# Two token groups share one pass over the gated layer's weights, the sign is set as a bit, and gate weights stay out of DRAM

## The chip, the cores and the metric

The kernel runs on one core of a Trainium2 chip. The metric is device time in microseconds (us), median of several runs. Before the change: 1014.65 us (three runs, 1012.99 to 1016.63).

## The reference, cut to what matters

Three layers follow each other on 4 x 576 = 2304 tokens of width 512: a causal attention with decay (8 heads of 64), a gated layer (SwiGLU, inner width 1536), and a top-1 mixture of 8 experts (inner width 1024).

```python
scores = where(causal, -1e9, q @ k.T / sqrt(64) + cum[:, None] - cum[None, :])
x = softmax(scores) @ v                       # per batch and head; then [2304, 512]
g = x @ w_gate                                # the gated layer
y = (g * sigmoid(g) * (x @ w_val)) @ w_out
logits = y @ r_gate                           # 8 experts
e = argmax(logits); gate = softmax(logits)[e]
out = gate * (relu(y @ w1[e]) @ w2[e])
```

Attention's inputs and the experts' weights are float32. `w_gate`, `w_val` and `w_out` arrive as float64 and are handed to the kernel as pairs of 32-bit words, so the kernel has to decode them into float32 itself.

## The kernel before, in words

**Stages.** Attention is cut into 64 *slots* (`slot`, line 446): 4 batches x 4 head pairs x 4 pieces. A slot computes scores (PE, lines 262 to 270), row maxima (DVE 317), exponentials (ACT 327), a float16 split of the probabilities (DVE 349 casts the high part, POOL 352 and 363 subtract the low part), a transpose by DMA (SP 366), and two slots later the product with v (PE 387). The 16 slots of one batch fill `xr`, the gated layer's input for 576 tokens.

**The gated layer** works in *units* (`unit`, from line 1101). A unit is a pair (group g of 256 tokens, column block j of 256 inner columns); there are 9 groups and NJ = 6 blocks, so 54 units. `unit_g` does 24 matmuls (line 503) and a tanh (ACT 526, DVE 529), `unit_v` 24 matmuls and the gating (DVE 536, ACT 542, POOL 543), and one unit later `unit_o` does 12 matmuls into two PSUM banks `yp` (line 556), which collect the six blocks of a group. When a group's last block is in, `fin0` copies the banks (ACT 589, DVE 590) to `ys` and stores them to the DRAM tensor `y_d`. The units run group by group: unit u is (u // 6, u % 6).

**Weights of the gated layer.** `decode` (line 869) makes float32 out of the 64-bit words: ACT 878 takes |hi| scaled by a power of two, ACT 879 writes the sign of hi over the raw words, DVE 880 shifts, DVE 881 ORs in the low word's top bits, POOL 884 multiplies by the sign. 36 tiles of 128 x 512 are decoded. The first 43 of the tasks (j = 0 to 4 of `w_gate` and `w_val`, and most of `w_out`) run between the first 18 slots; those of j = 5 come with the unit that needs them.

**Routing.** After a group's `fin0` its logits are formed: `fin1` (line 606) turns `ys` over, for groups 5 to 7 by splitting it into 16-bit words and a DMA transpose (`pair`, SP 620, then ACT 622 and DVE 623); `fin2` (line 638) computes logits, rank and gate weight on DVE and places them by small matmuls (PE 716). It also writes the gate weights, one 4-byte number per token, to the DRAM tensor `g_d` (SP, line 571, called from 735). At the end the overflow tile, for tokens beyond an expert's 320, gathers its gate weights from `g_d` by index (POOL 1366); so does a loop behind it, which runs only for further overflow tiles.

**What sets the order.** The program is recorded in Python order. A list scheduler then orders each engine's instructions. Each engine runs its queue in order; semaphores tie the queues together. The recorded order is steered by `pace`: a list `pts_` of (unit, slots done by then), between which slots are spread evenly. `upto(mark[j])` and `upto(markw[j])` force the decode tasks that a unit needs.

```python
pts_ = [(-1, first), (NJ - 2, first), (2 * NJ - 2, 8 * NP + 2), ...]   # line 1165: first = 18, NP = 4
```

So units 0 to 4 have no slots with them; the 16 slots of the second batch come with units 5 to 10.

Of the kernel before, what the change touches and what calls it, by code (L numbers as in the profile page):

```python
# [27 lines left out]
def kernel(  # L28
# [37 lines left out]
    g_d = dram.tile([NT + 1, 1], F32, name="g_d")  # L66
# [453 lines left out]

    def unit_g(u):
        g, j = divmod(u, KF // 2)
        gps = gv(g, j, 0, "g")
        t = M["t"].tile([128, 2, G], F32, tag="t", name="t")
        for b, c0, c1 in spans(g):
            act.activation(  # L526
                out=t[:, :, c0:c1], in_=gps[:, :, c0:c1], func=ACTF.Tanh, scale=gscale[:, b, j:j + 1]
            )
        vec.scalar_tensor_tensor(out=t, in0=t, scalar=1.0, in1=gps, op0=ALU.add, op1=ALU.mult)  # L529
        return t  # L530

    def unit_v(u, t):
        g, j = divmod(u, KF // 2)
# [12 lines left out]
    def unit_o(u):  # L546
        g, j = divmod(u, KF // 2)
        hi, lo = hbuf.pop(u)
        if j == 0:
            yps[g] = [ps_y.tile([128, DM], F32, tag=f"y{i}", name="yp") for i in range(2)]  # L550
        for i in range(2):
            n_ = 0
            for fi in range(2):
                fk = 2 * j + fi
                for hx, wx in ((hi, 0), (hi, 1), (lo, 0)):
                    pe.matmul(  # L556
                        out=yps[g][i],
                        lhsT=hx[:, fi, 128 * i:128 * i + 128],
                        rhs=wo[fk][wx],
                        start=(j == 0 and n_ == 0),  # L560
                        stop=(j == KF // 2 - 1 and n_ == 5),
                    )
                    n_ += 1
# [22 lines left out]

    def fin0(g):
# [50 lines left out]
    def fin2(g):  # L638
# [96 lines left out]
        rows_out(g_d, g, gw)  # L735
# [37 lines left out]
    def start():  # L773
# [25 lines left out]
        act.dma_start(out=g_d[NT:NT + 1, :], in_=zr[:, 0:1])  # L799
# [71 lines left out]
    def decode(src, n):  # L871
        c = c_tile()
        raw = fetch(src, n, c.rearrange("p (a n) -> p a n", a=n))
        if raw is not None:
            rv = raw.rearrange("p (m w) -> p m w", w=2)
            lo, hi = rv[:, :, 0], rv[:, :, 1]
            ci = c.bitcast(I32)
            act.activation(out=c, in_=hi.bitcast(F32), func=ACTF.Abs, scale=2.0 ** -112)
            act.activation(out=hi.bitcast(F32), in_=hi, func=ACTF.Sign)
            vec.tensor_single_scalar(out=ci, in_=ci, scalar=3, op=ALU.logical_shift_left)  # L880
            vec.scalar_tensor_tensor(
                out=ci, in0=lo, scalar=29, in1=ci, op0=ALU.logical_shift_right, op1=ALU.bitwise_or
            )
            gp.tensor_tensor(out=c, in0=c, in1=hi.bitcast(F32), op=ALU.mult)
# [37 lines left out]
    NJ = KF // 2  # L922
# [179 lines left out]
    def unit(u, between=None):  # L1102
# [62 lines left out]
    pts_ = [(-1, first), (NJ - 2, first), (2 * NJ - 2, 8 * NP + 2), (4 * NJ - 1, 12 * NP + 2), (6 * NJ - 2, NSL)]  # L1165
# [7 lines left out]
    for u in range(NU + 1):  # L1173
        if u < NJ:
            upto(mark[u])
        if u < NU and u % NJ == 0:
            for b, _, _ in spans(min(u // NJ + 1, NG - 1)):
# [4 lines left out]
        if u < NU:  # L1182
            need = 4 * NP * ((G * (u // NJ + 1) - 1) // S + 1) + 2
# [165 lines left out]

    def gate(s, t):  # L1350
# [60 lines left out]
    with tc.tile_pool(name="lw", bufs=1) as lw, tc.tile_pool(name="lr", bufs=3) as lr, tc.tile_pool(  # L1411
        name="lx", bufs=1
    ) as lx, tc.tile_pool(name="lp", bufs=2, space=PSUM) as lp:
        with tc.For_i(1, n_ov) as it:
# [4 lines left out]
            def lbank(tag):  # L1419
# [3 lines left out]
            gp.indirect_dma_start(  # L1423
                out=gwl, out_offset=None, in_=g_d[:, :],
                in_offset=bass.IndirectOffsetOnAxis(ap=idx.bitcast(U32), axis=0),
            )
# [18 lines left out]
            transp(xt, 0, xs, lbank)  # L1445
            hh, hl = [lx.tile([128, KF2, 128], F32R, name=f"lh{x}") for x in ("h", "l")]
# [33 lines left out]
```

## Time and profile before

| | |
|---|---|
| runs, median (lowest to highest) | 1014.65 us (1012.99 to 1016.63) |
| the profiled execution | 1012.41 us, of it 1010.6 us span |
| busy share of the span: PE, DVE, ACT, POOL | 87%, 61%, 55%, 39% |
| granted TensorE clock, mean | 0.943 |
| data moved by DMA | 146.35 MB, mean 145 GB/s |

The span is the time from the first to the last instruction of the profiled execution; 1.8 us lie around it. The profile's busy time counts work only, not waiting. An engine's average over the whole span hides the stages: up to about 173 us PE is mostly idle and the other engines and the DMAs are near full, after that PE is nearly always busy. The views used below are the table of busy time by stretch, groups of instructions by line, the waits, the chain of waits that ended last, and stretches of the timeline.

### The profile page before, as it was taken

The numbers are of one execution on the slowest core, as the hardware profiler recorded it, in microseconds if no ns is written. First come the engines' busy times: TensorE is split into PE (matmuls) and PEld (weight loads), VectorE is DVE, ScalarE is ACT, GpSimd is POOL, SyncE is SP. The second block draws the span as 40 slices with busy tenths as digits, with TensorE's granted clock in tenths as the row PEclk, the third lists the DMA queues.
The fourth block names the chain that finished last, engine by engine and source line by source line (L and its number), as shares of the span: only waits on it lengthen the run. The fifth ranks groups of instructions, "written<-read, shape, count | busy, mean of one in ns | idle before, by whom it ended". The sixth has DMA issues, their size and how long they took to land.

```text
span 1010.6 us, 19838 instructions
## 1 busy us (share of the span) xinstructions
PE 882.2 (87%) x7028; PEld 734.7 (73%) x7053; DVE 614.9 (61%) x1818; ACT 555.3 (55%) x1205; POOL 389.6 (39%) x467
## 2 busy tenths in 40 slices
PE   1545557998999989999999999898989999999995
PEld 0334336877777868888878888687869788889894
DVE  6999888487666746565644434334536675665540
ACT  5987988476677666665633322122425454555431
POOL 1468676464444425344442222222245632100101
PEclk9995657999999999999999999899989999999998
DMA  8897998347886787567545422112376887765420
GB/s 244 209 216 205 230 204 187 90 101 165 180 172 146 164 190 158 101 133 137 102 113 143 121 22 64 5 18 66 71 180 187 218 219 201 215 198 159 132 95 34
DMA packets 309481, 146.35 MB, mean 145 GB/s; under 512 B 273441, under 2 KB 285857, under 8 KB 309380
## 3 DMA queue, kind: packets, MB, share of 16 engines
q1 hardware_dynamic: 305088, 134.68, 56.2%
q0 software_dynamic: 4096, 10.24, 3.7%
q8 instruction: 56, 0.92, 0.4%
q14 instruction: 45, 0.37, 0.2%
q10 hardware_dynamic: 196, 0.14, 0.0%
HBM read 84.24 MB, written 10.31 MB: 94 GB/s over the span
## 4 chain that ended last, share of the span: by engine, by line
PE 46%; DMA 17%; issue 12%; DVE 6%; ACT 3%; SPq 2%; POOL 2%; POOLq 0%; DVEq 0%; ACTq 0%
PE yp L556 11%; PE g L503 10%; PE v L503 10%; DMA out_dram<-o,ix 5%; PE bank L1218 3%; DMA pt<-p 3%; PE px L387 2%; DMA pair<-yt 2%; PE bank L1261 2%; DMA pair<-words 2%; DMA wr<-in_moe_w_dram 1%; PE ps L262 1%; PE ps L263 1%; DVE wlo L978 1%; PE ps L265 1%
## 5 line engine op out<-in xcount | busy, mean ns | idle before, releaser
L352 POOL TENSOR_TENSOR p<-st,p 128x128 f16<-128x128 f32 (+3 forms) x128 | 110.1, 864 | 102.1 <-issue 62.7
L543 POOL TENSOR_TENSOR lo<-t,hi 128x512 fp32r<-128x512 f32 x54 | 70.1, 1299 | 149.3 <-ACT hi L542 121.6
L503 PE MATMUL g<-xr,wga 128*128 128x256 f16 x864 | 106.1, 277 | 0.3 <-DVE t L529 0.3
L503 PE MATMUL v<-xr,wva 128*128 128x256 f16 x864 | 106.2, 277 | 0.0
L327 ACT ACTIVATE st<-st,nb,c 128x64 f32<-128x64 f32 (+4 forms) x160 | 102.6, 643 | 0.9
L503 PEld LDWEIGHTS <-wga 128*128 128x128 f16 x864 | 82.6, 100 | 17.2 <-issue 6.6
L503 PEld LDWEIGHTS <-wva 128*128 128x128 f16 x864 | 84.8, 101 | 10.6 <-issue 0.3
L387 PE MATMUL px<-vs,pt 128*128 128x64 f16 x1280 | 56.3, 203 | 39.3 <-DMA pt<-p 28.8
L349 DVE CAST p<-st 128x64 f16<-128x64 f32 (+4 forms) x160 | 68.4, 442 | 31.6 <-ACT st L327 20.1
L317 DVE CUSTOM_DVE_ANT_0 st<-ps,zero 128x64 f32<-128x64 f32 (+3 forms) x160 | 55.8, 377 | 50.9 <-PE ps L270 48.8
L387 PEld LDWEIGHTS <-pt 128*128 128x128 f16 x1280 | 50.3, 105 | 49.3 <-DMA pt<-p 32.8
L363 POOL TENSOR_TENSOR p<-st,p 128x64 f16<-128x64 f32 (+1 forms) x128 | 54.1, 424 | 70.6 <-issue 36.4
L262 PE MATMUL ps<-qkt 128*128 128x64 f16 (+2 forms) x192 | 56.5, 312 | 21.1 <-DMA qkt<-qks 7.2
L526 ACT ACTIVATE t<-g,gscale 128x512 f32<-128x512 f32 (+3 forms) x72 | 39.4, 573 | 62.2 <-PE g L503 59.0
L1012 POOL DMA_INDIRECT out_dram<-o,ix x24 | 24.6, 1026 | 123.3 <-ACT o L1263 79.5
L542 ACT ACTIVATE hi<-t 128x512 fp32r<-128x512 f32 x54 | 33.8, 625 | 56.5 <-DVE t L536 56.5
L556 PE MATMUL yp<-wohi,hi 128*128 128x512 f32 x144 | 60.6, 421 | 0.0
L263 PE MATMUL ps<-qkt 128*128 128x64 f16 (+2 forms) x192 | 60.1, 315 | 0.0
L1223 ACT ACTIVATE h<-bank 128x320 fp32r<-128x320 f32 (+1 forms) x64 | 26.3, 422 | 60.1 <-PE bank L1218 59.8
L1225 DVE SCALAR_TENSOR_TENSOR h<-bank,h 128x64 fp32r<-128x64 f32 (+2 forms) x128 | 33.4, 305 | 40.4 <-ACT h L1223 40.4
L556 PE MATMUL yp<-wohi,lo 128*128 128x512 f32 x144 | 57.6, 402 | 0.0
L556 PE MATMUL yp<-wolo,hi 128*128 128x512 f32 x144 | 57.1, 397 | 0.0
(322 smaller groups left out, 2483.2 us busy)
## 6 DMA issues: line engine op xcount, KB each, us to landing
wr<-in_moe_w_dram SPq DMA_DIRECT2D x72, 512.0 KB, 5.1
vr<-in_v_dram SPq DMA_DIRECT2D x16, 288.0 KB, 4.5
qk_in<-in_q_dram SPq DMA_DIRECT2D x32, 128.0 KB, 2.5
qk_in<-in_k_dram SPq DMA_DIRECT2D x32, 128.0 KB, 2.6
v_in<-in_v_dram SPq DMA_DIRECT2D x32, 128.0 KB, 3.0
y_d<-ys SPq DMA_DIRECT2D x6, 512.0 KB, 3.5
wgb<-in_moe_w_gate_dram SPq DMA_DIRECT2D x5, 512.0 KB, 5.9
raw<-in_moe_w_val_dram SPq DMA_DIRECT2D x5, 512.0 KB, 4.2
```

The costliest lines, as they stand in the source:

```text
L262: pe.matmul(out=ps[:, o:o + n], lhsT=lq, rhs=qkt[:, 1, k0:k1], start=True, stop=False, skip_group_check=True)
L263: pe.matmul(out=ps[:, o:o + n], lhsT=lq, rhs=qkt[:, 2, k0:k1], start=False, stop=False, skip_group_check=True)
L317: vec.tensor_tensor_reduce(out=sts[m][:, k0 - 64:k1 - 64], in0=ps[:, o:o + n], in1=zero.to_broadcast([128, n]), scale=1.0, scalar=init, op ...
L327: act.activation(out=sts[m], in_=sts[m], func=ACTF.Exp, scale=c[:, 0:1], bias=nb[:, m:m + 1], accum_out=sm[:, m, hh:hh + 1],)
L349: vec.tensor_copy(out=flat[:, o + 64:o + 64 + n], in_=src)
L352: gp.tensor_tensor(out=flat[:, o1:o1 + n - 64], in0=src[:, 64:n], in1=flat[:, o + 128:o + 64 + n], op=ALU.subtract)
L363: gp.tensor_tensor(out=blk[:, :, 0:64], in0=pair, in1=blk[:, :, 64:128], op=ALU.subtract)
L387: pe.matmul(out=px[:, 128 * m + 64 * hh:128 * m + 64 * hh + 64], lhsT=pm[:, o + ph * last + c, :], rhs=vs[:, hh, c, vh, :], start=(c == 0 ...
L503: pe.matmul(out=ps[:, fi, :], lhsT=w16[:, kk, wi, 128 * fi:128 * fi + 128], rhs=xr[:, kk, x0:x0 + 2, xi, :], start=(n_ == 0), stop=(n_ == ...
L526: act.activation(out=t[:, :, c0:c1], in_=gps[:, :, c0:c1], func=ACTF.Tanh, scale=gscale[:, b, j:j + 1])
L543: last["lo"] = gp.tensor_tensor(out=lo, in0=t, in1=hi.bitcast(F32), op=ALU.subtract)
L556: pe.matmul(out=yps[g][i], lhsT=hx[:, fi, 128 * i:128 * i + 128], rhs=wo[fk][wx], start=(j == 0 and n_ == 0), stop=(j == KF // 2 - 1 and n ...
```

## The change

Four things change.

1. *The order of the units.* `order` replaces the division by six: (0,0), (0,1), (0,2), then all six of group 1, then (0,3), (0,4), (0,5), then groups 2 to 8 as before. Each column block is now used for both groups within nine units. The `yp` banks hold one group at a time, so the first half of group 0 is copied out (`part_out`) and stored to `y_d`; when the second half is done, `fin0(0)` loads it back and adds. The pools that the raw weights used are handed to routing after group 1 instead of group 0.
2. *The pace.* The point `(NJ - 2, first)` is gone: the 16 slots of the second batch are now spread over units 0 to 10.
3. *The sign.* ACT no longer writes a sign and POOL no longer multiplies; a third DVE instruction takes the sign bit of `hi` and ORs it in.
4. *Gate weights.* `g_d` is gone with its writes and its gathers. The overflow tile computes its gate weights again from its own turned rows (`gate_of`: eight matmuls of 128 x 8 and a short chain on DVE and ACT).

```diff
+    CUT = 3
+    NJ = KF // 2
+    order = (
+        [(0, j) for j in range(CUT)] + [(1, j) for j in range(NJ)] + [(0, j) for j in range(CUT, NJ)]
+        + [(g, j) for g in range(2, NG) for j in range(NJ)]
+    )
...
-        if j == 0:
+        opens = [0, CUT] if g == 0 else [0]
+        shuts = [CUT - 1, NJ - 1] if g == 0 else [NJ - 1]
+        if j in opens:
             yps[g] = [ps_y.tile([128, DM], F32, tag=f"y{i}", name="yp") for i in range(2)]
...
+    def part_out():
+        r = [c_p.tile([128, DM], F32, tag="c", name="yc") for _ in range(2)]
+        act.activation(out=r[0], in_=yps[0][0], func=ACTF.Copy)
+        vec.tensor_copy(out=r[1], in_=yps[0][1])
+        for i in range(2):
+            sp.dma_start(out=y_d[r0_of(i):r0_of(i) + 128, :], in_=r[i])
...
     def fin0(g):
         ys = M["y"].tile([128, 2, DM], F32, tag="ys", name="ys")
-        act.activation(out=ys[:, 0, :], in_=yps[g][0], func=ACTF.Copy)
-        vec.tensor_copy(out=ys[:, 1, :], in_=yps[g][1])
+        if g == 0:
+            rows_out(y_d, g, ys, True)
+            for i in range(2):
+                vec.tensor_tensor(out=ys[:, i, :], in0=ys[:, i, :], in1=yps[g][i], op=ALU.add)
+        else:
+            act.activation(out=ys[:, 0, :], in_=yps[g][0], func=ACTF.Copy)
+            vec.tensor_copy(out=ys[:, 1, :], in_=yps[g][1])
...
         vec.reciprocal(out=gw, in_=ge)
-        rows_out(g_d, g, gw)
...
-            act.activation(out=c, in_=hi.bitcast(F32), func=ACTF.Abs, scale=2.0 ** -112)
-            act.activation(out=hi.bitcast(F32), in_=hi, func=ACTF.Sign)
+            act.activation(out=c, in_=hi.bitcast(F32), func=ACTF.Copy, scale=2.0 ** -112)
             vec.tensor_single_scalar(out=ci, in_=ci, scalar=3, op=ALU.logical_shift_left)
             vec.scalar_tensor_tensor(
                 out=ci, in0=lo, scalar=29, in1=ci, op0=ALU.logical_shift_right, op1=ALU.bitwise_or
             )
-            gp.tensor_tensor(out=c, in0=c, in1=hi.bitcast(F32), op=ALU.mult)
+            vec.scalar_tensor_tensor(
+                out=ci, in0=hi, scalar=-2 ** 31, in1=ci, op0=ALU.bitwise_and, op1=ALU.bitwise_or
+            )
...
-    pts_ = [(-1, first), (NJ - 2, first), (2 * NJ - 2, 8 * NP + 2), (4 * NJ - 1, 12 * NP + 2), (6 * NJ - 2, NSL)]
+    pts_ = [(-1, first), (2 * NJ - 2, 8 * NP + 2), (4 * NJ - 1, 12 * NP + 2), (6 * NJ - 2, NSL)]
...
     for u in range(NU + 1):
-        if u < NJ:
-            upto(mark[u])
+        g, j = order[min(u, NU - 1)]
+        if u < 2 * NJ:
+            upto(mark[j])
...
+    def gate_of(xt, ps, pool, dst):
+        p = ps("t")[:, 0:NE]
+        prods = [(x, kk) for kk in range(KD) for x in xt]
+        for n_, (x, kk) in enumerate(prods):
+            pe.matmul(
+                out=p, lhsT=x[:, kk, 0:128].bitcast(F32), rhs=rg[:, kk, 0:NE], start=(n_ == 0),
+                stop=(n_ == len(prods) - 1), skip_group_check=True,
+            )
+        le = pool.tile([128, NE], F32, name="le")
+        vec.tensor_reduce(out=dst, in_=p, axis=AX.X, op=ALU.max)
...
-            gp.indirect_dma_start(
-                out=gwo, out_offset=None, in_=g_d[:, :],
-                in_offset=bass.IndirectOffsetOnAxis(ap=ixo.bitcast(U32), axis=0),
-            )
...
+                if nxt == NE:
+                    gate_of(xts[nxt % 2], bank, ix_p, gwo)
```

The queue of ACT where the second and third unit of group 0 run (L526 is a unit's tanh, L542 the copy that ends its gating; L878, L879, L895 belong to decode), before:

```order
L526 ACTIVATE t<-g,gscale 128x512
L878 ACTIVATE c<-raw 128x512
L879 ACTIVATE raw<-raw 128x512
L895 ACTIVATE wgb,totw<-c 128x4x128
L542 ACTIVATE hi<-t 128x512
```

The same place of the changed program (L532 and L548 are tanh and gating copy, L322 and L326 a slot's maxima and exponentials, L229 a slot's q and k, L207 a slot's constants, L395 its sums):

```order
L548 ACTIVATE hi<-t 128x512
L395 ACTIVATE sm<-sm,addc 128x4
L322 ACTIVATE nb<-mx,addc,c 128x3
L326 ACTIVATE st,sm<-st,nb,c 128x64
L326 ACTIVATE st,sm<-st,nb,c 128x192
L326 ACTIVATE st,sm<-st,nb,c 128x320
L207 ACTIVATE nc<-pick,c 128x256
L229 ACTIVATE qks<-qk_in_102,sc 128x5x64
L229 ACTIVATE qks<-qk_in_103,sc 128x2x5x64
```

Between two units' instructions there stand a slot's now, where decode alone stood.

The queue of SP where group 7 is turned over (L571 stores and loads rows, L620 is the DMA transpose of one half of `ys`, L968 loads an expert's weights), before:

```order
L571 DMA y_d<-ys 128x2x512
L620 DMA_TRANSPOSE pair<-yt 128x8x128
L571 DMA g_d<-gw 128x1 x2
L620 DMA_TRANSPOSE pair<-yt 128x8x128
L968 DMA wr<-in_moe_w_dram 128x1024 x2
L571 DMA g_d<-gw 128x2x1
```

The same place of the changed program (L579 is line 571 of before, L643 line 620, L989 line 968):

```order
L579 DMA y_d<-ys 128x2x512
L643 DMA_TRANSPOSE pair<-yt 128x8x128 x2
L989 DMA wr<-in_moe_w_dram 128x1024 x4
L989 DMA wr<-in_moe_w_dram 128x2x512 x3
L579 DMA y_d<-ys 128x2x512
```

The second transpose follows the first, where two writes of gate weights stood between them; the same holds for group 6, where three stood.

The queue of POOL early in the decode (L884 is the multiplication by the sign, L352 and L363 a slot's low parts), before:

```order
L884 TENSOR_TENSOR wo<-wo,wgb 128x512
L884 TENSOR_TENSOR wo<-wo,wvb 128x512
L352 TENSOR_TENSOR p_2_109<-st,p_2_109 128x384
L363 TENSOR_TENSOR p_2_109<-st,p_2_109 128x64
L352 TENSOR_TENSOR p_3_110<-st,p_3_110 128x512
```

The queue of DVE early in the decode of the changed program (L900 is line 880 of before, L901 line 881, L904 the added instruction):

```order
L900 TENSOR_SCALAR wo<-wo 128x512
L901 SCALAR_TENSOR_TENSOR wo<-wvb,wo 128x512
L900 TENSOR_SCALAR wo<-wo 128x512
L904 SCALAR_TENSOR_TENSOR wo<-wvb,wo 128x512
L901 SCALAR_TENSOR_TENSOR wo<-wgb,wo 128x512
```

The third step of a decode has moved from the queue of POOL into that of DVE; DVE's queue holds 28 of the 36 before the last instruction that fills `xr` for the first batch, where 30 of L881 stood.

## Rows read from the trace of the kernel before

**Rows 1.** Busy time by stretch: stretch, length, PE, PEld, DVE, ACT, POOL, clock, DMA
```profile
0.00:25.00 25.00, 2.93 (x10) 2.50 (x10) 15.80 (x55) 14.88 (x33) 4.46 (x15) 1.00 0.86 244
25.00:100.00 75.00, 39.51 (x320) 27.91 (x324) 71.27 (x199) 65.73 (x162) 47.96 (x54) 0.82 0.85 208
100.00:173.00 73.00, 45.03 (x390) 33.85 (x390) 62.87 (x173) 65.58 (x165) 49.34 (x55) 0.62 0.94 216
173.00:203.00 30.00, 28.57 (x231) 24.06 (x228) 16.25 (x27) 14.96 (x29) 14.53 (x11) 1.00 0.33 87
203.00:300.00 97.00, 90.64 (x891) 72.30 (x896) 70.08 (x231) 68.86 (x176) 49.58 (x69) 0.98 0.70 155
300.00:371.00 71.00, 65.67 (x686) 53.21 (x687) 47.76 (x156) 48.99 (x129) 31.49 (x47) 0.98 0.76 159
371.00:546.00 175.00, 173.46 (x1729) 145.60 (x1739) 97.66 (x317) 99.03 (x249) 72.79 (x104) 1.00 0.62 130
```

**Rows 2.** Busy time up to 173 us of line 884 (POOL) alone
```profile
0.00:173.00 173.00, 41.29 (x29) 0.76 0.89 216
```

**Rows 3.** The same of line 879 (ACT)
```profile
0.00:173.00 173.00, 19.37 (x30) 0.76 0.89 216
```

**Rows 4.** The same of line 880 (DVE)
```profile
0.00:173.00 173.00, 19.22 (x30) 0.76 0.89 216
```

**Rows 5.** The same of line 881 (DVE)
```profile
0.00:173.00 173.00, 25.13 (x30) 0.76 0.89 216
```

**Rows 6.** Lines 880 and 881: duration ns, shortest/median/longest
```profile
L880 DVE TENSOR_SCALAR c<-c x19: 408/427/1519, 14.4 to 215.4; 128x512 int32<-128x512 int32 x19
L881 DVE SCALAR_TENSOR_TENSOR c<-raw,c x10: 674/693/1656, 14.9 to 217.3; 128x512 int32<-128x512 int32 x10
```

**Rows 7.** Timeline of POOL and DVE near 174 us: start, us, engine, line
```profile
173.74 1.48 POOL L884 TENSOR_TENSOR c<-c,wvb 128x512 f32<-128x512 f32 x1
...
174.15 1.62 DVE L881 SCALAR_TENSOR_TENSOR c<-raw,c 128x512 int32<-128x512 int32 x1
```

**Rows 8.** Waits of SP's queue up to 173 us: total us, times, longest
```profile
SPq L366 <- POOL wo L884: 4.7, 3, 2.9
SPq L366 <- POOL c L884: 4.3, 2, 3.4
```

**Rows 9.** Busy time by stretch where the clock is at half
```profile
636.60:643.40 6.80, 6.17 (x21) 4.96 (x22) 2.22 (x7) 1.18 (x3) 2.43 (x3) 0.50 0.00 0
698.00:701.40 3.40, 3.40 (x15) 2.63 (x15) 2.17 (x4) 0.25 (x1) 0.21 (x1) 0.50 0.47 128
230.40:233.80 3.40, 3.40 (x12) 1.87 (x12) 3.40 (x14) 3.40 (x11) 2.00 (x4) 0.50 0.52 118
```

**Rows 10.** The chain that ended last, 600 to 715 us: start, us, what
```profile
616.25 2.75 PE yp L556 x12
...
626.55 9.21 DMA pair<-yt
...
650.80 2.52 PE yp L556 x11
...
669.30 2.51 PE yp L556 x11
...
678.77 2.75 PE yp L556 x12
...
689.30 6.31 DMA pair<-yt
...
709.93 2.75 PE yp L556 x12
```

**Rows 11.** Timeline near 636 us; in brackets the idle time before and its releaser
```profile
637.23 1.09 PE L716 MATMUL rk<-rb,ra 128*128 128x48 f32 x4 [4.72 <-DVE rb L736]
```

**Rows 12.** From issue to landing: all writes of `g_d`
```profile
DMA to landing us min/median/max: 6.2/7.7/9.6
```

**Rows 13.** From issue to landing: the transpose issued at 621.0 us
```profile
DMA to landing us min/median/max: 3.1/3.1/3.1
```

More of the change, by code (lines that the diff above doesn't have):

```diff
@@ L65 @@
     y_d = dram.tile([NT + 1, DM], F32, name="y_d")
-    g_d = dram.tile([NT + 1, 1], F32, name="g_d")
     id_d = dram.tile([NSLOT, 1], I32, name="id_d")
@@ L519, in spans @@
         return r
+    CUT = 3
[4 more added lines that the diff above has]
+    )
     def unit_g(u):
-        g, j = divmod(u, KF // 2)
+        g, j = order[u]
         gps = gv(g, j, 0, "g")
@@ L532, in unit_v @@
     def unit_v(u, t):
-        g, j = divmod(u, KF // 2)
+        g, j = order[u]
         vps = gv(g, j, 1, "v")
@@ L546, in unit_o @@
     def unit_o(u):
-        g, j = divmod(u, KF // 2)
+        g, j = order[u]
         hi, lo = hbuf.pop(u)
-        if j == 0:
+        opens = [0, CUT] if g == 0 else [0]
+        shuts = [CUT - 1, NJ - 1] if g == 0 else [NJ - 1]
+        if j in opens:
             yps[g] = [ps_y.tile([128, DM], F32, tag=f"y{i}", name="yp") for i in range(2)]
@@ L559, in unit_o @@
                         rhs=wo[fk][wx],
-                        start=(j == 0 and n_ == 0),
-                        stop=(j == KF // 2 - 1 and n_ == 5),
+                        start=(j in opens and n_ == 0),
+                        stop=(j in shuts and n_ == 5),
                     )
@@ L585, in rows_out, with r0_of @@
                 put_rows(dst[r0[i]:r0[i] + 128, :], src[:, i, :])
+    def part_out():
[4 more added lines that the diff above has]
+            sp.dma_start(out=y_d[r0_of(i):r0_of(i) + 128, :], in_=r[i])
+    def r0_of(c):
+        return 128 * c + 64
     def fin0(g):
         ys = M["y"].tile([128, 2, DM], F32, tag="ys", name="ys")
-        act.activation(out=ys[:, 0, :], in_=yps[g][0], func=ACTF.Copy)
-        vec.tensor_copy(out=ys[:, 1, :], in_=yps[g][1])
+        if g == 0:
[5 more added lines that the diff above has]
+            vec.tensor_copy(out=ys[:, 1, :], in_=yps[g][1])
         rows_out(y_d, g, ys)
@@ L798, in start @@
         act.dma_start(out=y_d[NT:NT + 1, :], in_=zr)
-        act.dma_start(out=g_d[NT:NT + 1, :], in_=zr[:, 0:1])
     def pow2_scale(dst, inv, parts):
@@ L920, in wo_dec @@
         gp.tensor_tensor(out=lo, in0=t, in1=hi.bitcast(F32), op=ALU.subtract)
-    NJ = KF // 2
     tasks, mark, markw = [], {}, {}
@@ L1108, in unit @@
         if u > 0:
-            if u - 1 < NJ:
-                upto(markw[u - 1])
+            g1, j1 = order[u - 1]
+            if g1 < 2:
+                upto(markw[j1])
             unit_o(u - 1)
-            g1, j1 = divmod(u - 1, NJ)
+            if (g1, j1) == (0, CUT - 1):
+                part_out()
             if g1 == NG - 1 and j1 < len(EP["w2"]):
@@ L1123, in unit @@
             if j1 == NJ - 1:
-                if g1 == 0:
+                if g1 == 1:
                     sg.close()
@@ L1173 @@
     for u in range(NU + 1):
-        if u < NJ:
-            upto(mark[u])
-        if u < NU and u % NJ == 0:
-            for b, _, _ in spans(min(u // NJ + 1, NG - 1)):
+        g, j = order[min(u, NU - 1)]
+        if u < 2 * NJ:
+            upto(mark[j])
+        if u < NU and (u == 2 * NJ - 1 or u % NJ == 0 and u >= 2 * NJ):
+            for b, _, _ in spans(min((u + 1) // NJ + (u % NJ == 0), NG - 1)):
                 if b not in unscaled:
@@ L1182 @@
         if u < NU:
-            need = 4 * NP * ((G * (u // NJ + 1) - 1) // S + 1) + 2
+            need = 4 * NP * ((G * (g + 1) - 1) // S + 1) + 2
         tgt = pace(u)
@@ L1348, in turn @@
         split(xt[0][:, :, 0:o], xt[1][:, :, 0:o], xf[:, :, 0:o], xt[0][:, :, 0:o].bitcast(F32))
+    def gate_of(xt, ps, pool, dst):
[8 more added lines that the diff above has]
+        vec.tensor_reduce(out=dst, in_=p, axis=AX.X, op=ALU.max)
+        vec.tensor_tensor(out=le, in0=p, in1=dst.to_broadcast([128, NE]), op=ALU.subtract)
+        act.activation(out=le, in_=le, func=ACTF.Exp)
+        vec.tensor_reduce(out=dst, in_=le, axis=AX.X, op=ALU.add)
+        vec.tensor_single_scalar(out=dst, in_=dst, scalar=1e-9, op=ALU.add)
+        vec.reciprocal(out=dst, in_=dst)
     def gate(s, t):
@@ L1422 @@
             gwl = lx.tile([128, 1], F32, name="gwl")
[L1423 to L1426, printed above, removed]
             xs = gather(lx, [idx])
@@ L1445 @@
             transp(xt, 0, xs, lbank)
+            gate_of(xt, lbank, lx, gwl)
             hh, hl = [lx.tile([128, KF2, 128], F32R, name=f"lh{x}") for x in ("h", "l")]
```

## The prediction

> **What bounds the kernel now.** I read the table of busy time by stretch first, then the groups by line for the instructions that go, then the waits, and the chain of waits for what is left. In the table [rows 1] the reader is to see two kernels behind each other. Up to 173 us PE works 87.5 us and waits 85.5; DVE works 15.80 + 71.27 + 62.87 = 149.94, ACT 146.2, POOL 101.8, and the DMAs are 85 to 94% full. DVE is the fullest of the four: 95% of 25 to 100 us (71.27 of 75), 86% of 100 to 173 us. From 173 us on PE is the bound: it idles 1.43 us up to 203, 6.36 in the next 97 (6.6%), 5.33 in the next 71 (7.5%), and only 1.54 in the 175 behind them (0.9%). So an instruction more on DVE costs time ahead of 173 us and nothing behind it, and behind it only what stops PE, or its clock, counts. Two places stop it later: the chain [rows 10] goes twice through a DMA transpose `pair<-yt` of 9.21 and 6.31 us.
>
> The profiled execution took 1012.41 us (span 1010.6 and 1.8 around it); the median of the runs is 1014.65, 2.2 above. I sum against the profiled execution and add 2.2 at the end.
>
> **Term 1, the decode up to 173 us.** Removed there: 29 multiplications on POOL, 41.29 us, 41% of its 101.8 [rows 1, 2], and 30 sign activations on ACT, 19.37 us [rows 3]. Added: a DVE instruction per tile. Its kind (two tensors in, shift or mask and OR) is that of line 881, which takes 0.693 us as its median, 25.13 / 30 = 0.84 as its mean [rows 5, 6]. By its order, 28 tiles are decoded there where 30 were, so 28 x 0.69 = 19.3 to 28 x 0.84 = 23.5 us are added, and two tiles of lines 880 and 881, 2 x (0.64 + 0.84) = 3.0 us [rows 4, 5], go out: +16.3 to +20.5.
>
> Against that stands what POOL does to DVE. A `L881` that starts at 174.15 takes 1.62 us instead of 0.69; it ends 0.55 us after the multiplication on POOL that was under way has ended (173.74 + 1.48 = 175.22) [rows 7]. Over the stretch, line 880 takes 19.22 - 30 x 0.427 = 6.4 us more than by its median and line 881 25.13 - 30 x 0.693 = 4.3 us more [rows 4 to 6]. If all of these 10.7 us were due to the instruction that goes, DVE's net load rises by 16.3 - 10.7 = 5.6 us; if none, by 20.5. Other DVE instructions beside it would shorten too, and their share is not in these rows. I take +5, near the lower end, because rows 7 show this very pair and because the instruction that goes is the largest of POOL's.
>
> The Trainium skill ("SBUF — State Buffer", section "Who interferes with whom") says that DVE's second pair of ports is GpSimd's too and is locked for the whole instruction, a DVE instruction with two SBUF inputs among those that collide. Rows 7 agree; and the rule speaks against the change too, since the added instruction has two SBUF inputs and the slots' subtractions on POOL stay. By it alone the price would be the stalled mean, 0.84 us, for each of the 28.
>
> If DVE stays the bound and is 95% full from 25 us on, the first batch ends at 25 + (71.27 + 62.87 + x) / 0.95 = 166.2 + x / 0.95: x = 5 gives 171.5, x = 20.5 gives 187.8. ACT has 19.4 us less in its way, and SP's queue no longer waits 4.7 + 4.3 = 9.0 us for multiplications on POOL with the slots' transposes behind them [rows 8]. What is late next is DVE, and behind it the DMAs (0.89 x 173 = 154 us of full load). I take **-2 us**, between -9 (all of SP's wait back) and +15.
>
> **Term 2, 173 to 371 us.** The 16 slots of the second batch stand beside units 0 to 10 instead of 5 to 10, 1.5 to a unit instead of 2.7. They hold work for PE, which no longer lies crowded, and whose chain through DVE, ACT, POOL and a transpose gets more room. PE idles 1.43 + 6.36 = 7.8 us in 173 to 300 us [rows 1]. At the 0.9% of the later stretch it would be 1.1 us, at the crowded rate it stays; I take 3%, 3.8 us, so -4. In the crowded stretch the granted clock also falls once to 0.50, the 1.2 GHz level, for 3.40 us, though PE worked all of it [rows 9]; at 2.4 GHz that work takes half: -1.7 if the drop goes. The 5.33 us at 300 to 371 I leave, since the slots there move little. Moved with the units: `part_out` puts one copy on ACT, one on DVE and two stores on SP, `fin0(0)` a load and two DVE additions in place of two copies; ACT and DVE have 28 and 27 us to spare in 203 to 300 us, and the stores go out nine units ahead of the load's use; that costs nothing unless the load, waiting in SP's queue, holds up a slot's transpose behind it. The other order of the units makes no matmul more or less. Term 2: **-6 us**, between -13 (both stretches at 0.9%, two drops of the clock gone) and +5 (units 0 to 4, 46 us at 9.25 each, idle 7.5% instead, 3.5 us, and one drop more).
>
> **Term 3, the writes of `g_d`.** A transpose with no such write ahead of it lands 3.1 us after its issue [rows 13]; one behind three of them takes 9.21, one behind two 6.31 [rows 10], and the writes themselves 6.2 to 9.6 [rows 12]: 4-byte pieces, one a token. Behind it, PE waits 4.72 us for `rb`, the last step of a chain on DVE that begins with that transpose [rows 11], and the clock is then at 0.50 for 6.80 us; after the second it is so for 3.40 us [rows 9]. The whole loss comes from the chain [rows 10]: the outer matmuls at 650.80 and 669.30 are two units apart, 9.25 us a unit. From 616.25 to 650.80 there are three units, 27.75 us, in 34.55: 6.8 lost. From 678.77 to 709.93 again three, in 31.16: 3.4 lost. If the transposes land in 3 to 4 us, PE does not stop and its clock does not fall: **-10 us**, between 0 and -10.2.
>
> The Trainium skill ("DMA: Bandwidth & Descriptors", section "Queues, rings and completion order") says that a transfer's semaphore increment is an ordered write that lands only after every earlier write of that DMA engine, across its queues. Rows 10, 12 and 13 agree; by the rule the lateness goes with the writes, and if rows 10 have another cause, Term 3 is nothing.
>
> **Term 4, the tail.** `gate_of` adds eight small float32 matmuls for PE and a short chain on DVE and ACT. The nearest row is four float32 matmuls in 1.09 us, 0.27 each [rows 11]: 8 x 0.27 = 2.2 us at most, with far fewer columns here; at least 0. I take **+1 us**. Its DVE and ACT steps lie beside the overflow tile's matmuls, and the gathers that go are taken at nothing.
>
> **Sum.** -2 - 6 - 10 + 1 = -17: 1012.4 - 17 = 995.4, by the runs' median 997.6.
>
> **The rivals.**
>
> A. *DVE eats the gain.* The added instruction is never relieved, because the subtractions on POOL take the place that the multiplication left: x = 20.5, Term 1 is +15, and 15 - 6 - 10 + 1 = 0: 1014.6. For it: DVE is 95% full in 25 to 100 us. Against it: POOL falls from 101.8 to 60.5 us.
>
> B. *Slower: DVE bounds the slots into the units.* All 36 tiles cost 0.84 us (30.2), none is relieved, and DVE, held by slots and decode in one queue, fills no more than the 86% of 100 to 173 us up to the end of group 1. Up to 300 us it now works 149.94 + 16.25 + 70.08 = 236.3; with 30 more, 25 + (266.5 - 15.8) / 0.86 = 316 us instead of 300: +16, and 16 - 10 + 1 = +7: 1021.6. It decides as soon as the added load passes (300 - 25) x 0.86 + 15.8 - 236.3 = 16 us. Against it: DVE is only 72% full in 203 to 300 us, which leaves it 27 us.
>
> C. *The transposes stay late.* They share the DMAs with experts' weights; if that makes them late, -2 - 6 + 1 = -7: 1007.6. For it: in the order such loads stand right behind the transposes. Against it: 3.1 us without a write ahead [rows 13], and the more writes ahead, the later [rows 10].
>
> D. *Both early terms at their best*: -9 - 13 - 10 + 1 = -31: 983.6. For it: the waits of SP are on the way of the transposes. Against it: DVE must then take its added load for nothing.
>
> **Chances.** Forecast 0.52, with a range of its own of 988 to 1007; A 0.18, B 0.13, C 0.12, D 0.05. A measurement of this kernel can tell about 0.3%, 3 us, from no change. Faster holds the forecast, C, D and a quarter of A (0.05): 0.74. Same is most of A: 0.11. Slower is B and what of A goes past 3 us: 0.15. The range reaches from D to A, 982 to 1014; B lies outside it.
>
> **What the next profile would show.** Term 1: PE is full from 171 us on instead of 173, DVE over 90% busy up to there, the new instruction at 0.69 to 0.84 us as its mean, line 880's mean below 0.64, and no wait of SP for a multiplication. A mean above 0.84 and a full PE only from 180 us on is A. Term 2: PE's idle time between the first unit and the end of group 1 near 4 us, and no stretch at 0.50 there; over 10 us, with DVE over 85% busy, is B. Term 3: `pair<-yt` landing in 3 to 4 us in groups 6 and 7, no wait of PE for `rb`, no half clock behind it; transposes over 6 us are C. Term 4: eight matmuls under 2.2 us together. The prediction is wrong if the transposes stay late, or if the first unit starts later than before by more than 10 us.

## The result and the profile after

The changed kernel takes 989.8 us (median of four runs, 989.49 to 990.25) against 1015.64 before; the ratio is 0.9745, with a 95% interval of 0.9717 to 0.9774. The forecast was 997.6, range 982 to 1014. The profiled execution has a span of 987.8 us where 1010.6 stood: 22.8 us less (the profiled execution of before, 1012.41 us, was 3.2 us quicker than its kernel's median by now). The same table of busy time by stretch, of the kernel after:

```profile
0.00:25.00 25.00, 3.58 (x17) 3.14 (x18) 17.60 (x58) 14.52 (x31) 1.89 (x13) 1.00 0.87 218
25.00:100.00 75.00, 39.63 (x323) 27.74 (x322) 68.64 (x202) 59.38 (x149) 31.67 (x40) 0.63 0.90 214
100.00:173.00 73.00, 49.53 (x429) 35.10 (x429) 68.10 (x210) 59.36 (x153) 31.90 (x42) 0.65 1.01 224
173.00:203.00 30.00, 28.98 (x288) 23.42 (x286) 25.88 (x73) 23.81 (x60) 19.20 (x27) 1.00 0.85 160
203.00:300.00 97.00, 88.49 (x844) 72.10 (x842) 69.23 (x210) 65.01 (x160) 39.30 (x54) 0.96 0.83 170
300.00:371.00 71.00, 69.72 (x694) 57.77 (x694) 40.76 (x128) 43.46 (x113) 29.85 (x41) 1.00 0.73 141
371.00:546.00 175.00, 173.59 (x1722) 145.38 (x1721) 98.78 (x316) 97.81 (x244) 72.33 (x101) 1.00 0.59 125
```

Against [rows 1], POOL has fallen from 101.8 to 65.5 us up to 173 us and ACT from 146.2 to 133.3; DVE has risen from 149.94 to 154.34. From 100 to 173 us the DMAs' share is now 1.01 where it was 0.94 (a packet counts whole where it starts, so a share can pass 1).

Where the 22.8 us lie is read from two matmuls of the chain. In [rows 10] the product of a unit starts at 616.25, and nine units later at 709.93. The same two in the chain of the kernel after (start, us, what):

```profile
610.82 2.75 PE yp L564 x12
...
692.30 2.75 PE yp L564 x12
```

Up to the first 616.25 - 610.82 = 5.4 us are gained. Between them 93.68 us have become 81.48: 12.2 gained. Behind them 1010.6 - 709.93 = 300.7 have become 987.8 - 692.30 = 295.5: 5.2 gained.

**Up to 370 us.** The two stretches that matter end with the product of the first unit and with that of the seventeenth. Before:

```profile
0.00:181.12 181.12, 94.16 (x783) 69.67 (x789) 157.67 (x438) 152.08 (x368) 109.85 (x128) 0.77 0.87 211
181.12:369.98 188.86, 177.17 (x1723) 143.23 (x1730) 126.35 (x399) 126.92 (x321) 86.50 (x121) 0.98 0.67 148
```

After:

```profile
0.00:176.77 176.77, 96.50 (x788) 68.97 (x789) 158.11 (x476) 135.74 (x336) 69.22 (x99) 0.70 0.94 218
176.77:364.50 187.73, 176.92 (x1731) 144.91 (x1730) 131.46 (x399) 125.67 (x317) 83.04 (x116) 0.98 0.78 157
```

Length less busy time is PE's idle time: 86.96 us in the first stretch have become 80.27, and 11.69 in the second 10.81. The first stretch itself is 4.4 us shorter: PE's busy time in it grew by 2.3 us, at a mean clock of 0.70 for 0.77. So the early gain lies ahead of the first unit, and the second stretch is nearly unchanged.

**Behind group 7.** PE no longer waits for `rb`, of which [rows 11] hold the longer of two waits. The two largest of PE's waits from 540 to 770 us before (us, times, longest):

```profile
PE rk L716 <- DVE rb L736: 7.3, 2, 4.7
PE bank L1091 <- DMA xg<-y_d,ix: 3.9, 1, 3.9
```

The second of them had not been in the forecast: the tail's first gather of tokens. All waits of PE after, from 540 to 760 us:

```profile
PE bank L1242 <- ACT xh L92: 0.5, 1, 0.5
PE bank L1112 <- DMA xg<-y_d,ix: 0.5, 2, 0.3
```

In the chain before, this gather takes 7.41 us, right behind the write of group 8's gate weights, and the clock is at half behind it:

```profile
745.18 7.41 DMA xg<-y_d,ix
```

```profile
752.60:759.40 6.80, 6.20 (x29) 5.72 (x30) 1.71 (x3) 1.89 (x4) 4.50 (x5) 0.50 0.78 226
```

In the chain after, where no write precedes it:

```profile
729.91 3.44 DMA xg<-y_d,ix
```

The transposes of `pair`, from issue to landing (all six; [rows 10] had 9.21 and 6.31 us in the chain), after:

```profile
DMA to landing us min/median/max: 3.1/3.4/5.0
```

How far these two readings hold is seen over the traces of all fourteen kernels (the change, before and the runs below). Units 37 to 54 (from the end of the 36th unit's product to that of the last), beside which the transposes lie, take 165.3 to 174.3 us in the five kernels with the 4-byte writes and 155.6 to 156.3 us in the nine without, the changed kernel among them (155.9, against 168.0 before). The part behind the last unit, the tail, is not so clear: 274.9 to 283.0 us with the writes, 272.9 to 282.2 us without, and the changed kernel has the shortest, 272.9. What goes with the writes there is the wait for the gather: PE's longest idle time ahead of the matmuls that turn gathered rows (line 1091 of before) is 3.0 to 6.1 us with them and 0.2 to 1.9 us without. The half clock goes with them less surely: all five have 6.8 us of it or more some 20 us into the tail, but of the nine without, e8_old_order has as much there (6.80 us from 733.9 us on), and e1_no_gd and e10_gd_one_piece have 3.40 us.

### The profile page after: what moved, and what is told of

It reads as the page before. It is cut to its first block, busy times and chain, and to the rows that moved or that the text cites. A ratio compares the mean times of both kernels' runs of the same rounds, so it can differ in the third digit from the quotient of the medians.

```text
span 987.8 us, 19793 instructions
## 1 busy us (share of the span) xinstructions
PE 878.5 (89%) x7069; PEld 731.9 (74%) x7069; DVE 622.1 (63%) x1861; ACT 538.6 (55%) x1170; POOL 344.0 (35%) x430
## 4 chain that ended last, share of the span: by engine, by line
PE 40%; DMA 10%; issue 9%; DVE 2%; ACT 1%; POOL 1%; SPq 0%; POOLq 0%; DVEq 0%; ACTq 0%
PE yp L564 11%; PE v L502 10%; PE g L502 9%; DMA out_dram<-o,ix 5%; DMA pair<-words 2%; PE bank L1242 2%; PE bank L1285 2%; PE px L386 1%; DMA wr<-in_moe_w_dram 1%; DMA pt<-p 1%; DVE wlo L999 1%; DMA xg<-y_d,ix 1%; PE ps L261 1%; PE ps L264 1%; PE ps L262 1%
## 5 line engine op out<-in xcount | busy, mean ns | idle before, releaser
L502 PE MATMUL g<-xr,wga 128*128 128x256 f16 x864 | 103.8, 274 | 9.3 <-ACT xr L439 8.4
L326 ACT ACTIVATE st<-st,nb,c 128x64 f32<-128x64 f32 (+4 forms) x160 | 102.8, 644 | 1.7
L362 POOL TENSOR_TENSOR p<-st,p 128x64 f16<-128x64 f32 (+1 forms) x128 | 58.2, 455 | 116.7 <-issue 37.0
L348 DVE CAST p<-st 128x64 f16<-128x64 f32 (+4 forms) x160 | 60.1, 385 | 33.1 <-ACT st L326 30.0
L532 ACT ACTIVATE t<-g,gscale 128x512 f32<-128x512 f32 (+3 forms) x72 | 39.4, 572 | 74.3 <-PE g L502 73.7
L548 ACT ACTIVATE hi<-t 128x512 fp32r<-128x512 f32 x54 | 33.7, 624 | 52.1 <-DVE t L542 52.1
L264 PE MATMUL ps<-cum,nc 128*128 128x64 bf16 (+2 forms) x192 | 58.8, 312 | 0.0
```

What stands on the lines that cost most here:

```text
L264: pe.matmul(out=ps[:, o:o + n], lhsT=pk, rhs=cum3[:, k0 - 64:k1 - 64], start=False, stop=(k1 <= d0), skip_group_check=True,)
L326: act.activation(out=sts[m], in_=sts[m], func=ACTF.Exp, scale=c[:, 0:1], bias=nb[:, m:m + 1], accum_out=sm[:, m, hh:hh + 1],)
L348: vec.tensor_copy(out=flat[:, o + 64:o + 64 + n], in_=src)
L362: gp.tensor_tensor(out=blk[:, :, 0:64], in0=pair, in1=blk[:, :, 64:128], op=ALU.subtract)
L502: pe.matmul(out=ps[:, fi, :], lhsT=w16[:, kk, wi, 128 * fi:128 * fi + 128], rhs=xr[:, kk, x0:x0 + 2, xi, :], start=(n_ == 0), stop=(n_ == ...
```

## The experiments

All ratios are to the kernel before, run beside them; it took 1016.20 us beside e1 to e4, 1013.71 beside e6 to e9 and 1013.35 beside e10 to e13. Differences in us below are between medians, across these groups too; by the ratios a distance from the changed kernel comes out up to 2.3 us larger (in the first group up to 1.4 us smaller). The first eight, in the table, undo or do the parts alone.

| kernel | gate weights out of DRAM | sign as a bit | new pace | new order | median us | ratio (95%) |
|---|---|---|---|---|---|---|
| e1_no_gd | yes | | | | 1001.25 | 0.9856 (0.9825 to 0.9888) |
| e2_sign | | yes | | | 1015.51 | 0.9997 (0.9977 to 1.0017) |
| e3_order_pace | | | yes | yes | 1009.6 | 0.9927 (0.9907 to 0.9946) |
| e4_gd_back | writes alone put back | yes | yes | yes | 1004.33 | 0.9874 (0.9855 to 0.9894) |
| e6_old_pace | yes | yes | | yes | 1004.43 | 0.9908 (0.9880 to 0.9937) |
| e7_no_gd_sign | yes | yes | | | 999.0 | 0.9857 (0.9830 to 0.9884) |
| e8_old_order | yes | yes | yes | | 992.7 | 0.9789 (0.9766 to 0.9812) |
| e9_no_sign | yes | | yes | yes | 1000.71 | 0.9873 (0.9852 to 0.9894) |
| the change | yes | yes | yes | yes | 989.8 | 0.9745 (0.9717 to 0.9774) |

**e1_no_gd: gate weights out of DRAM alone.** The edit is the fourth part of the diff and nothing else.

> Before with the fourth part alone: no writes or gathers of gate weights, gate_of in the tail. Theory T (the writes cost three places: the transposes of groups 6 and 7 and the first gather of tokens behind group 8, 7.9 + 4.3 + 5.2 us in the two traces): about 17 us faster than before, near 998, transposes `pair<-yt` landing in 3 to 5 us, no half clock near 636, 698 and 752 us. Rival R (the prediction's own term, the transposes alone, 10 us less 1 for the tail): 9 us faster, about 1006. Rival C (other traffic makes them late): within 3 us of before.

Measured: 1001.25, some 15 us faster. No half clock stands near the transposes, and PE waits for nothing in these groups. The third place came out in part only: the tail is 2.9 us shorter than before, not 5.2, and still has 3.40 us at half clock from 743.1 us on. The fourth part alone is more than half of the gain, and more than the forecast's 10 less 1.

**e4_gd_back: the writes put back, read by nobody.**

```diff
...
         vec.reciprocal(out=gw, in_=ge)
+        rows_out(g_d, g, gw)
```

> The changed kernel with the twelve writes of gate weights put back as they stood, read by nobody. Theory T: about 17 us slower than the changed kernel, near 1007, with half clock behind the transposes of groups 6 and 7 and behind the first gather of the tail. Rival (what went with the gathers or with gate_of brought part of it, not the writes): less than 10 us slower.

Measured: 1004.33, 14.5 us slower than the changed kernel. It is the writes: gathers and `gate_of` are as in the changed kernel. PE waits for `rb` again (its waits, 540 to 735 us):

```profile
PE rk L740 <- DVE rb L760: 6.5, 2, 4.5
```

and the chain goes again through late transfers:

```profile
620.77 6.43 DMA pair<-yt
...
677.59 8.47 DMA pair<-yt
```

The clock is at half for 6.8 us behind the transposes of group 7 and behind the tail's first gather, as expected, but not behind those of group 6.

**e10_gd_one_piece: as many small writes, each in one piece.** The source is one row of `rb`, 384 contiguous bytes (14 writes by the trace; the expectation's twelve is a miscount). The places are not the old ones: `rb` is ready later than `gw`, so the writes come behind the second transpose of groups 6 and 7, where those of e4_gd_back stand ahead of it (from 618.91 us on, the transpose at 620.77). At group 6 (start, us of the issue):

```profile
617.49 1.25 SPq L644 DMA_TRANSPOSE pair<-yt  x1
623.48 0.82 SPq L764 DMA_DIRECT2D g_d<-rb  x3
```

```diff
...
+        for i in range(3 if mix_ else 1 if r0_[1] == r0_[0] + 128 else 2):
+            sp.dma_start(out=g_d[3 * g + i:3 * g + i + 1, :], in_=rb[0:1].rearrange("p a b s -> p (a b s)"))
```

> The changed kernel with twelve small writes at the places of the old ones, each one contiguous piece of 384 bytes instead of 64 to 256 pieces of 4 bytes; read by nobody. If the many 4-byte pieces are what delays the transfers behind them: within 3 us of the changed kernel, 988 to 993, transposes `pair<-yt` landing in 3 to 5 us. If any write ahead does it: near 1004, as with the old writes, and transposes of 6 to 9 us.

Measured: 994.82, ratio 0.9805 (0.9783 to 0.9826), 5 us above the changed kernel and 9.5 below the old writes. PE has no wait for `rb`; but as no write stands ahead of a transpose, the run does not test what one in one piece would do there. For the tail's gather it does: the write of group 8 is issued at 723.98 us, the first gather at 725.15, and PE's waits for its rows from 540 to 735 us are short:

```profile
PE bank L1120 <- DMA xg<-y_d,ix: 0.2, 1, 0.2
PE bank L1120 <- issue: 0.2, 1, 0.2
```

Whether any write ahead makes a transpose late is settled by the trace of before. Three stores of `ys` stand right ahead of the transpose that lands in 3.1 us ([rows 13]):

```profile
618.30 2.57 SPq L571 DMA_DIRECT2D y_d<-ys  x3
620.97 1.32 SPq L620 DMA_TRANSPOSE pair<-yt  x1
```

The same function cuts these and the gate weights' writes into 256 rows a group; a row is 2048 bytes here and 4 bytes there. So it is the writes of 4-byte pieces that make the transposes late, and not any write ahead, nor the number of rows alone. Against the changed kernel the profile of e10 is 2.2 us ahead at the end of the last unit and loses 9.3 us in the tail, where PE waits 6.5 us for `h` (3.8 in the changed kernel) and the clock is at half in two stretches, 3.40 and 10.20 us long. Why the tail is so here stays open.

**e11_gd_on_act: the writes on ACT's queue.**

```diff
...
+        rows_out(g_d, g, gw, eng=act)
```

> The changed kernel with the twelve writes of gate weights put back, but issued from ACT's queue instead of SP's. If the delay sits in the DMA engines that both queues use: near 1004, as with the writes on SP's queue. If it sits in SP's own queue: within 3 us of the changed kernel, 988 to 993.

Measured: 1017.52, ratio 1.0036 (1.0012 to 1.0061): 28 us slower than the changed kernel, worse than with the writes on SP's queue. The transposes, still on SP, are late in three groups now:

```profile
565.92 8.12 DMA pair<-yt
...
625.33 7.99 DMA pair<-yt
...
684.76 9.22 DMA pair<-yt
```

```profile
PE rk L740 <- DVE rb L760: 13.5, 3, 6.0
```

The delay is thus not one of SP's own queue; it goes across queues. Of the 11.6 us by which this profile is longer than that of e4_gd_back, 8.9 lie in units 37 to 54, with the third late transpose: its write is issued beside it, at 566.12 us, where on SP's queue it stood behind (567.05, the transpose at 565.71). The other 2.9 lie in the tail and stay open.

**e2_sign: the sign alone.** The edit is the third part of the diff.

> Before with the sign as a bit alone. Theory T (the stretch up to 173 us ends 5.4 us earlier because of the sign, and nothing else moves it): 4 to 6 us faster, about 1010; the last copy into xr near 164 us instead of 169.3; DMA share of 100 to 165 us near 1. Rival A (DVE pays for the third instruction, and it is the units' order that brought the 5.4 us): 0 to 15 us slower, last copy into xr at 169 us or later.

Measured: no difference, 0.9997. Theory T fell, and so did rival A: the first unit's product ends at 169.11 us, 12 us earlier, and the seventeenth's 6.8 us later.

```profile
0.00:169.11 169.11, 87.97 (x725) 65.79 (x731) 148.23 (x450) 130.56 (x324) 65.86 (x91) 0.73 0.94 219
169.11:376.76 207.65, 186.66 (x1779) 149.72 (x1787) 140.17 (x424) 131.68 (x332) 87.72 (x123) 0.96 0.70 141
```

PE's idle time is 81.14 and 20.99 us: 5.8 gained in the first stretch, 9.3 lost in the second. It gave back what it won.

**e3_order_pace: order and pace alone.**

> Before with the order of the units and the pace alone (sign by ACT and POOL, gate weights in DRAM as before). Theory T: within 2 us of before, since PE's stalls from the first unit to the end of unit 16 sum to the same in both traces. Rival (the prediction's second term): 4 to 6 us faster, PE's idle time between 173 and 300 us near 4 us instead of 7.8. Rival A: all of the 5.4 us come from here.

Measured: 1009.6, 0.7% faster. Its profiled run is the slowest of its six (1014.8), and there the seventeenth unit ends at 370.14 us and PE idles 10.8 us between the two products, both as before; where the faster runs gain is not seen. Without the writes of gate weights the same two parts bring nothing (e9_no_sign against e1_no_gd), so I build nothing on it.

New theory P: the sign saves waiting ahead of the first unit, but only slots that start with the first units let the earlier start pay. The next four runs test it.

**e6_old_pace: the changed kernel with the old pace.**

```diff
-    pts_ = [(-1, first), (2 * NJ - 2, 8 * NP + 2), ...]
+    pts_ = [(-1, first), (NJ - 2, first), (2 * NJ - 2, 8 * NP + 2), ...]
```

> The changed kernel with the old pace (no slots beside its first units). The sign alone moved nothing, though PE's first unit ended 12 us earlier with it: PE then waited 9 us more in units 1 to 16, where the slots of the second batch are crowded. Theory P (the pace is what lets the early start pay): near 1000, PE's waits in units 1 to 16 near 20 us. Rival O (the order of the units does it: the decode of blocks 3 to 5 gets later): within 3 us of the changed kernel, 987 to 993.

Measured: 1004.43, 14.6 us slower than the changed kernel. As theory P expected, the first stretch stays short and the second gets PE's waits:

```profile
0.00:175.10 175.10, 95.69 (x741) 67.95 (x747) 155.77 (x468) 133.98 (x331) 66.50 (x96) 0.70 0.92 217
175.10:378.34 203.24, 183.09 (x1766) 148.12 (x1772) 136.27 (x406) 127.78 (x321) 88.52 (x120) 0.97 0.73 147
```

Idle: 79.41 and 20.15 us. PE waits there for slots; against the changed kernel, which has 7.8 us for `pt` and 0.7 for `qkt`, it is the wait for `qkt`, a slot's q and k, that has grown:

```profile
PE px L386 <- DMA pt<-p: 7.6, 9, 1.6
PE ps L261 <- DMA qkt<-qks: 7.1, 5, 2.6
```

**e8_old_order: the changed kernel with the old order of the units.**

> The changed kernel with the old order of the units (and the new pace). Theory P: within 3 us of the changed kernel, 987 to 993. Rival O: near 1000.

Measured: 992.7. PE's idle time is 77.98 and 11.40 us, as in the changed kernel (80.27 and 10.81), and the seventeenth unit ends at 364.10 us where the changed kernel has 364.50.

```profile
0.00:176.58 176.58, 98.60 (x783) 70.11 (x789) 158.38 (x478) 136.93 (x338) 67.53 (x98) 0.69 0.94 220
176.58:364.10 187.52, 176.12 (x1721) 144.44 (x1730) 131.99 (x395) 124.01 (x315) 86.14 (x117) 0.98 0.77 150
```

The order of the units, the first in the list of changes, gives nothing there. The 3 us by which the medians differ (the intervals overlap) lie in the tail of the profiles, where this kernel's profile has a stretch at half clock (733.9 to 740.7 us) that the changed kernel's lacks; what the order has to do with it stays open. So a worth of the new order is not shown. Without the pace (e6_old_pace against e7_no_gd_sign) it costs about 5 us; the two intervals just touch. With the old order the pace is worth 6.3 us (e7_no_gd_sign against e8_old_order, of one group, intervals apart).

**e7_no_gd_sign and e9_no_sign.**

> Before with the sign as a bit and gate weights out of DRAM (old order of units, old pace). If the sign by itself is worth nothing whatever else stands: 1001, as with gate weights out of DRAM alone. If the sign was worth something that the writes hid: 995 or less.

> The changed kernel with the sign by ACT and POOL again. With gate weights in DRAM, order and pace brought 6.6 us and sign, order and pace together 12.8; if the same holds here, the sign is worth 5 to 6 us behind the new order and pace: 995. If the parts only add up (the sign worth nothing): 990.

Measured: 999.0 and 1000.71; e1_no_gd had 1001.25. The sign without pace and order brings nothing sure, pace and order without the sign nothing, all three together 11.5 us. Taking the sign back costs 10.9 us, not the 5 to 6 expected. In the profile of e7_no_gd_sign the first unit ends 7.3 us earlier than before and the seventeenth at the same time, as theory P has it, though PE's idle time between them grows to 14.9 us only, not to 20:

```profile
0.00:173.82 173.82, 94.85 (x742) 67.91 (x747) 156.13 (x464) 134.53 (x332) 69.11 (x96) 0.71 0.93 217
173.82:369.59 195.77, 180.83 (x1763) 147.83 (x1772) 131.99 (x409) 127.06 (x319) 80.95 (x117) 0.97 0.68 141
```

PE's idle time in e9_no_sign is 87.89 and 10.37 us: the pace's short second stretch stays, and the sign's 8 us ahead of the first unit are gone. At the end of the seventeenth unit it is 4.5 us behind the changed kernel; 3.9 us more are lost in the tail, with 6.8 us at half clock, and that loss is not traced to the sign.

```profile
0.00:184.14 184.14, 96.25 (x786) 70.12 (x793) 162.99 (x467) 157.33 (x385) 112.42 (x131) 0.70 0.90 212
184.14:369.02 184.88, 174.51 (x1721) 143.71 (x1728) 130.35 (x372) 121.54 (x305) 91.48 (x120) 0.98 0.78 157
```

**e12_pool_work and e13_act_work: which engine's relief is it?** The first adds, per tile, a multiplication on POOL whose result nobody reads; the second a sign activation on ACT. Both write a scratch tile `jnk`.

```diff
...
+            gp.tensor_tensor(out=jnk, in0=c, in1=c, op=ALU.mult)         # e12_pool_work
...
+            act.activation(out=jnk, in_=hi, func=ACTF.Sign)              # e13_act_work
```

> The changed kernel with a multiplication on POOL per decoded tile, whose result nobody reads (128 x 512, two float32 inputs, bfloat16 output), so POOL's load of before without its place in the chain. If the sign's gain ahead of the first unit (8 us less idle PE) comes from DVE being free of that work: 5 to 11 us slower than the changed kernel, 995 to 1001, with the mean of the decode's DVE instructions up by a tenth or more. If it comes from ACT's load or from the shorter chain: within 3 us.

> The changed kernel with a sign activation on ACT per decoded tile, whose result nobody reads: ACT's load of before without its place in the chain. If ACT's 19 us were what the sign gave ahead of the first unit: 5 to 11 us slower than the changed kernel. If it was POOL beside DVE, or the chain: within 3 us.

Measured: 1010.28, ratio 0.9969 (0.9948 to 0.9989), and 1000.52, ratio 0.9873 (0.9849 to 0.9897): 20.5 and 10.7 us slower than the changed kernel. The first stretch of the one and of the other:

```profile
0.00:201.23 201.23, 104.01 (x846) 73.27 (x847) 185.35 (x511) 149.02 (x368) 111.99 (x139) 0.68 0.82 198
```

```profile
0.00:185.54 185.54, 97.66 (x823) 71.36 (x824) 164.22 (x512) 161.93 (x399) 74.72 (x107) 0.71 0.89 212
```

PE idles 97.2 and 87.9 us where the changed kernel has 80.3. At the end of the seventeenth unit the first is 16.1 us behind the changed kernel (380.55 us) and the second 4.0 (368.47). Each loses 6 us more in the tail, where the added work does not run; why stays open.

POOL's work acts in two ways, which the run does not separate. SP's queue, which issues the slots' transposes, waits 11.4 us for it up to 201 us, as it waited 9.0 us for the sign's multiplications ([rows 8]). And DVE is 92% full. Its decode steps and casts get longer. The shift (line 901 there) and the cast (line 348) up to 173 us:

```profile
0.00:173.00 173.00, 17.89 (x29) 0.64 0.83 205
0.00:173.00 173.00, 20.90 (x43) 0.64 0.83 205
```

The same two in the changed kernel (lines 900 and 348):

```profile
0.00:173.00 173.00, 15.57 (x29) 0.69 0.94 219
0.00:173.00 173.00, 16.28 (x47) 0.69 0.94 219
```

0.62 us a shift against 0.54, and 0.49 a cast against 0.35, with a tenth fewer casts done. ACT's work costs too: with it back the ratio is 0.9873, as without the sign altogether (e9_no_sign), so nothing of the sign's gain is left. The expectations, which took it to be the one engine or the other, were wrong in their "or".

## Why the prediction was right, and where it was not

**Term 1, the decode.** The load of DVE came out near the sum: 154.34 - 149.94 = 4.4 us more up to 173 us, where 5 was taken. It did so by other instructions than the sum counted. The shift fell from 19.22 us for 30 tiles ([rows 4]) to 15.57 for 29, the OR from 25.13 ([rows 5]) to 22.54 (the first row below): 0.16 us a tile, 4.8 us in all, less than half of the 10.7 us of stall. As much and more came from the casts, which the sum had left out: 23.74 us for 46 before (the second row) and 16.28 for 47 after.

```profile
0.00:173.00 173.00, 22.54 (x29) 0.69 0.94 219
0.00:173.00 173.00, 23.74 (x46) 0.76 0.89 216
```

The new instruction, up to 173 us:

```profile
0.00:173.00 173.00, 22.07 (x29) 0.69 0.94 219
```

22.07 / 29 = 0.76 us, between the 0.69 and 0.84 of the bounds. The gain was taken too small, -2, because the step "if DVE stays the bound" made DVE alone set the end. Measured it is 6.7 us less idle PE ahead of the first unit, and e12_pool_work and e13_act_work show why: POOL's load, put back alone, costs 17 us of idle PE there, and ACT's alone 7.6, each as much as the whole gain or more. ACT's 19 us, to which the sum gave no time of their own, count too. The DMAs are full there as well, with a share of 1.01; whether they now set the end was not tested.

**Term 2, the pace.** -6 was forecast against the kernel before, by PE's waits falling from 7.8 to 3.8 us. They did not: 9.5 us from 173 to 300 us, 11.69 and 10.81 us in the second stretch, and the clock falls twice as it did before (230 and 360 us there):

```profile
239.70:243.10 3.40, 3.40 (x19) 2.42 (x17) 2.73 (x15) 2.90 (x9) 3.00 (x6) 0.50 0.52 116
273.80:277.20 3.40, 3.40 (x28) 2.60 (x26) 2.90 (x17) 2.10 (x7) 1.46 (x2) 0.50 0.33 69
```

The forecast took the fall of the clock to come though PE worked. But each of these falls stands within 2 us behind a wait, here for a slot's transpose (before, a wait of 1.86 us ends at 229.54 us, the fall is at 230.40):

```profile
237.81 0.58 PE L386 MATMUL px<-vs,pt 128*128 128x64 f16 x14 [2.62 <-DMA pt<-p]
...
272.54 0.49 PE L386 MATMUL px<-vs,pt 128*128 128x64 f16 x11 [2.45 <-DMA pt<-p]
```

The waits stayed, and the falls with them. (The term's lower end is also mis-summed: with two falls gone it is -14.7, not -13.) The step that failed is the assumption that the four parts add. The pace does not shorten the waits of before; it keeps an earlier start from lengthening them, to 15 us in e7_no_gd_sign and 20 us in e2_sign and e6_old_pace. Terms 1 and 2 together were -8 and came to -5.4.

**Term 3, the writes.** -10 at these two places became -12.2; PE's wait for `rb` went as forecast. e4_gd_back and e11_gd_on_act show that the writes are the cause, on either queue, and not the experts' weights (rival C); the stores of `ys` ahead of a transpose that is not late show that it takes the 4-byte pieces. The rule of the Trainium skill ("DMA: Bandwidth & Descriptors", section "Queues, rings and completion order"), that a transfer's increment lands only after earlier writes of its DMA engine, across queues, agrees with e11_gd_on_act: 7.99 to 9.22 us for transposes on SP behind or beside writes on ACT's queue.

**Term 4, the tail.** +1 became -5.2: the largest miss. `gate_of` stayed within its bound of 2.2 us, eight matmuls of a quarter microsecond:

```profile
L1378 PE MATMUL bank<-rg,xh x8: 171/256/257, 939.1 to 940.5; 128*128 128x8 f32 x8
```

But Term 3 stopped at the transposes. The write for group 8 stood ahead of the tail's first gather in the same way, and PE waited 3.9 us for it. I had read the chain only up to 715 us. Of the 5.2 us the 3.4 of this wait (3.9 to 0.5) are shown to be the write's. The 6.8 us at half clock behind it may be in part: e8_old_order has as much there without a write. That the changed kernel has none there, and the shortest tail of all, was in no term of the forecast and is luck as far as these runs go.

**The sum.** Terms 1 to 3 were -18 and came to -17.6. That they come so near is luck too: Term 2 was 5 us too much, Terms 1 and 3 were some 2 us too little each.

**Rivals.** A and B did not come: DVE was relieved, if in the casts more than in the two lines that were counted. B's price is real all the same: with POOL's work kept beside the third instruction (e12_pool_work) nearly the whole change is lost.

## What to carry to other kernels

A tiny scattered store can cost nothing where it is issued; look behind it for every transfer, on any queue, that an engine waits for, to the end of the program. An earlier start pays only if the work that comes after it is also handed out earlier, so two edits that each measure nothing can be worth 1% together, and neither may be judged alone. Where several engines are near full, taking work off one can be worth little unless the next one is relieved too, as e13_act_work shows beside e9_no_sign: put dummy work back on each to see which counts.

## What the runs showed of the hardware that was not expected

- 4-byte pieces delay a transfer on another queue: 64 to 256 of them in a write on ACT's queue put transposes issued by SP to 7.99 to 9.22 us from 3.1 to 5.0, while three stores of 256 rows of 2048 bytes in all, the last issued 0.7 us ahead of a transpose, leave it at 3.1 us.
- At 239.70 and 273.80 us (above) the granted clock falls to 0.50 for 3.40 us, and PE is busy through all of them. In both places PE had just waited, 2.62 and 2.45 us, and was back at work for 1.9 and 1.3 us when the clock fell.
- A multiplication on POOL whose result nobody reads, together with the waits that it brings, goes with longer casts on DVE, which write float16 from one input: 0.49 us in the mean for 0.35.
